# Output weights loaded in parts, one multiplication moved on ScalarE, and a new order at the end, in a fused attention and squared-ReLU kernel

## The chip, the cores and the metric

The kernel runs on one core of one Trainium2 chip, in float32. The metric is the device time of one execution in microseconds (us). A profiled execution gives a trace of every instruction; its span runs from the first instruction of the program to the last.

## The reference

```
# q, k, v: (8, 12, 448, 64); g_q, g_k: (64,)
q_n, k_n = rmsnorm(q, g_q), rmsnorm(k, g_k)       # x / sqrt(mean(x*x) + 1e-6) * g
attn = softmax(q_n @ k_n.T / 8)                    # per batch and head, 448 x 448
x = (attn @ v).transpose(0, 2, 1, 3).reshape(3584, 768)
h = maximum(x @ w_in, 0)                           # w_in: 768 x 2048
out = (h * h) @ w_out                              # w_out: 2048 x 768
```

Eight batches of twelve heads go through attention; their 3584 rows go through a feed-forward network with a squared ReLU.

## The kernel before

**Attention** works on pairs of heads: 48 pairs (six in each batch), two heads of 64 side by side on 128 partitions. For a pair, q and k are scaled by their root mean square, transposed (on TensorE for early pairs; for later ones by block-wise DMA loads and a transpose on VectorE, `turn_blocks`, L364), and q is then multiplied by the gains g on ScalarE (L369). TensorE makes scores (`score`, L429), ScalarE takes exponentials (`weigh`, L451, the instruction is L454), and TensorE multiplies these with v (`attend`, L518, with the matmuls L550 and L571 for late pairs). Late pairs are "whole": they are handled in one visit (`visit_whole`, L1772), in which scores, exponentials and the attend step of the pair before alternate on TensorE and ScalarE.

**The feed-forward network** works in four units `u` of two batches each. Matrix products are done with seven products in place of eight (Strassen's scheme, in Winograd's form). A unit has four blocks; a block has a first product (x times w_in, 128 x 224 pieces, L1042, from unit 1 on with two levels of the scheme, `deep_products`, L1013) and a second product (hidden times w_out, 128 x 384 pieces, L1251, `second_products`, L1205). The second product needs eight "forms" of two tiles of w_out, named 11, 12, 21, 22, T1 to T4; they are made once, in unit 0, kept in DRAM (`out_forms`), and loaded again for each block of units 1 to 3 by `load_out` (L899, the DMA is L902). One load is 128 x 3072 floats, 1536 KB; two make up a block.

The seven products of a row tile are P1 to P7, in an order given by lists (`SECOND_ORDER` and others, L916 on). Each product is added to accumulators by ScalarE or VectorE (`add_to`, L1339, with the addition L1345). P1 and P2 make the upper left part c11, P1, P6, P5 and P3 the upper right c12, P7 adds to both lower parts c21 and c22. After the last block the accumulators are stored by SP (`store`, L1346, the DMA is L1350). Units 1 and 2 ("KEPT", "split") spread their second product over five PSUM banks, and keep 64 rest rows of each batch for unit 3, which handles them as one more row tile, `tt == NT`, the last of four in each block. Their operands come from DRAM by `bring_rests` (L1181).

**The order of the work** is written out by a planner in Python: `ffn` (L943) is a generator that yields after each product with a cost; `run` (L1586) draws from it up to a planned cost, and between draws gives out other work: attention tasks, and DMA issues that were put into `later` with a countdown of steps (`follow_loads`, L1535). `visit_whole` and the visits like it stand between two stretches of `run`. At the end of a unit (`x == unit`, L1851) `drain` gives out all tasks that are left, and then the next unit's generator is begun. [...]nearly all DMAs are issued by SP, in one queue.

Of the kernel before, what the change touches and what calls it, by code (L numbers as in the profile page):

```python
# [225 lines left out]
def program(ctx, tc, rows, v, g, wide, ones, moe_w_in, moe_w_out, out, shift):  # L226

    nc = tc.nc

    B, H, S, D = v.shape  # L230
    NPAIR = H // 2
    DM, DFF = moe_w_in.shape
    NC = DM // P
    NF = DFF // P
# [42 lines left out]
    def whole(i):  # L277
        return i > 2 * 2 * NPAIR
# [30 lines left out]
    def room_for_blocks(i, x):  # L309
        return rows.room(i)[:, x].rearrange("p g h d -> p (g h d)")[:, ds(i % 2 * S, S)]  # L310
# [53 lines left out]
    def turn_blocks(i, x):  # L364
        ensure("blocks", i, x)
        dst = att.tile([P, S], F32, name="qT" if x == 0 else "kT")
        nc.vector.transpose(dst, room_for_blocks(i, x))  # L367
        if x == 0:
            nc.scalar.mul(dst, dst, g)  # L369
        turned[i, x] = dst  # L370

    def load_v(i):
        b, c = pairs[i]
# [321 lines left out]

    def leave(i):
        b, c = pairs[i]
        for x in range(2):
            del turned[i, x]
        del values[i]  # L700
        if b == 1:
            begin_forms(c)
        elif b > 1:
            settle(b, c)
# [191 lines left out]
        side, place = divmod((n * 10 + PLACES[m]) % (2 * SIDE_OF_RING), SIDE_OF_RING)  # L896
        return ring[side][:, place]

    def load_out(n):  # L899
        if NF // 2 <= n < B // 2 * NF // 2:  # L900
            out_sb[n] = new_out()
            nc.sync.dma_start(out_sb[n], out_forms[n % (NF // 2)])  # L902

    roles = [banks[n] for n in (7, 6, 5)]

    def turn_roles(*order):
# [9 lines left out]
    FIRST_ORDER = ["P1", "P5", "P2", "P6", "P3", "P4", "P7"]  # L916
    FIRST_OF_BLOCK = ["P1", "rest0", "P5", "P4", "P6", "P2", "rest1", "P3", "P7"]
    SECOND_ORDER = ["P1", "P2", "P5", "P6", "P4", "P3", "P7"]
    SPLIT_ORDER = [
# [285 lines left out]
    def second_products(u, blk, hid, sums_, accs):  # L1205
# [20 lines left out]
                yield len(some) * COST_OUT  # L1226
            turn_roles(2, 1, 0)

        def store_rows(tt, e):
            if tt is None or tt == NT:  # L1230
                n = u if tt is None else KEPT[e]
                parts = [(2 * n, P * NT, REST), (2 * n + 1, 0, REST)]
            else:
                parts = [(2 * u + e, REST * e + P * tt, P)]
            store(accs[-1] if tt is None else accs_of(tt)[e], parts)

        def accs_of(tt):
            return extra["accs"] if tt == NT else accs[2 * tt : 2 * tt + 2]
# [48 lines left out]
        def store_some(name):  # L1287
            if name in ("P2", "P4") and blk == NBLK - 1:
                while to_store:
                    store_rows(*to_store.popleft())  # L1290

        if split:
            places = [*roles, banks[1], banks[2]]
            for name, tt, n in SPLIT_ORDER:
# [9 lines left out]
                if tt:  # L1304
                    store_some(name)
                yield COST_OUT
        for tt in range(0 if split else NT + final):
            order = SECOND_ORDER if tt or not u else FIRST_OF_BLOCK
            for name in order:
                if name.startswith("rest"):  # L1310
                    a = int(name[-1])
                    multiply_rest(
                        u, blk, hid, banks[2:0:-1], PARTS_BY_ROW[2 * a : 2 * a + 2],
                        accs[-1] if a else None,
                    )
                    if a:
                        held.discard("others")
                    yield 2 * COST_OUT
                    continue
                ps = roles[PRODUCTS[name][0]][:, 0:HALF]  # L1320
                product(tt, name, ps, nc.scalar if order is SECOND_ORDER else nc.vector)
                if name == "P1" and order is FIRST_OF_BLOCK:
                    yield from sums_behind_first()
                    continue
                if order is not FIRST_OF_BLOCK:
                    store_some(name)
                yield COST_OUT
            turn_roles(2, 0, 1)
        while to_store and blk == NBLK - 1:
            some = to_store.popleft()  # L1330
            if final:
                store_rows(*some)
            else:
                later.append([2, lambda some=some: store_rows(*some)])
        for n in ns:
            del out_sb[n]
        later.append([4, lambda: [load_out(n + 2) for n in ns]])

    def add_to(acc, ps, first=False, engine=nc.scalar):  # L1339
        if first and engine is nc.scalar:  # L1340
# [2 lines left out]
            nc.vector.tensor_copy(out=acc, in_=ps)  # L1343
        else:
            nc.vector.tensor_tensor(out=acc, in0=acc, in1=ps, op=ALU.add)  # L1345
    def store(acc, parts):  # L1346

        at = 0
        for b, row, n in parts:
            nc.sync.dma_start(out[ds(b * S + row, n), :], acc[at : at + n, :])  # L1350
            at += n


# [181 lines left out]
    def follow_loads():  # L1535

        for some in to_load:
            some[0] -= 1
        while to_load and to_load[0][0] <= 0:
            load_weights(to_load.popleft()[1])  # L1540
        for some in later:
            some[0] -= 1
        while later and later[0][0] <= 0:
            later.popleft()[1]()

# [224 lines left out]
            tasks.append(lambda: load_blocks(i, 1))  # L1770

    def visit_whole(i):  # L1772
        late = [some for some in tasks if getattr(some, "args", None) == (i,)]
        for some in late:
            tasks.remove(some)
        run_all()
        if shift:
            attend_all(i - 1)
            if i <= last:
                weigh_slots(i, 1)  # L1780
        else:
            if i % 2 == 0:
                both_denominators(i - 2)
            for n in range(NJ):
                attend(i - 1, (n,))
                forget(i - 1, (n,))
                if i <= last:
                    score(i, n)
                    weigh(i, n)
                while n == 1 and i % 2 == 0 and late:  # L1790
                    late.pop(0)()
            if i % 2:
                attend(i - 1, (NJ,))
                forget(i - 1, (NJ,))
            join_halves(i - 1)
            if i % 2 == 0:
                tasks.append(lambda: invert_both(i - 2))
                if i <= last:
                    score(i, NJ)
                    weigh(i, NJ)  # L1800
            if i <= last:
                additions(i)
        tasks.extendleft(reversed(late))
        if late:
            tasks.extendleft([gap] * 3)
        if shift or i % 2:
            prepare(i + 3)
        else:
            tasks.append(lambda: tasks.append(lambda: prepare(i + 3, 0)))
        if i <= last:  # L1810
            tasks.appendleft(lambda: load_v(i))
# [7 lines left out]
    with tc.manual_schedule(engines=ENGINES):  # L1819
        if shift:  # L1820
            rows.scale(0, 1, nc.gpsimd)
        turn(0, 1)
        turn(0, 0)
        for x in range(2):
            rows.normalize_first(1, x, new_acc()[:, 0 : 4 * P])
        if shift:
            rows.scale(1, 1, nc.gpsimd)
        for i in range(len(pairs) + 1):
            for n in range(1 if whole(i) else VISITS):
                at = i * VISITS + n - VISITS - unit  # L1830
                if at < 0:
                    visit_alone(i, n)
                    continue
                u, x = divmod(at, unit)
                if x == 0:
                    u, x = u - 1, unit
                run(place(u, x - (1 if whole(i - 1) else 0.5)))
                if i < last:
                    if whole(i) and not shift:
                        tasks.append(partial(lambda i: turn_blocks(i + 1, 1), i))  # L1840
                        tasks.append(partial(lambda i: turn_blocks(i + 1, 0), i))
                        tasks.append(partial(lambda i: load_qk(i + 4), i))
                    else:
                        for some in (1, 0) if whole(i) else (1 - n,):
                            turn_among(i + 1, some)
                        if n or whole(i):
                            tasks.append(lambda i=i: load_qk(i + 4))
                    if n and first and x > 1 and not shift:
                        denominators(i - 1)
                run(place(u, x))  # L1850
                if x == unit:  # L1851
                    drain()
                    stream, spent, first = ffn(u + 1), 0, u < 0
                    if shift:
                        run(COST if first else LATER)
                    elif first:
                        run(COST_IN + 1)
                slowly = x < unit
                if whole(i):
                    visit_whole(i)  # L1860
                else:
                    visit_among(i, n)
        run(LATER)
        drain()
        assert not transfers
        for _ in ffn(B // 2 - 1):
            follow_loads()
            follow_plan(1)
# [29 lines left out]
```

## Time and profile before

| what | value |
|---|---|
| median of 3 runs | 1393.48 us (1393.12 to 1394.81) |
| the profiled execution's own time | 1394.38 us |
| its span | 1392.6 us |
| TensorE (PE) busy | 1363.3 us, 98% |
| ScalarE (ACT) busy | 608.3 us, 44% |
| VectorE (DVE) busy | 807.2 us, 58% |
| GpSimd (POOL) busy | 789.6 us, 57% |
| moved by DMA | 233.36 MB, mean 168 GB/s |
| granted TensorE clock | 0.998 of full speed |

PE stands for matmuls, PEld for weight loads, SPq for SP's queue of DMA issues. One float32 matmul shows as two records. In a timeline line the first number is the start in us from the span's start, the second how long the line's records lasted together, then engine, line of the kernel, operation, output and inputs with shapes, the number of records, and in brackets how long the engine stood idle before the first and what released it. In the list of costliest groups the numbers behind the bar are busy us, mean ns of one, and idle us before the group. In the list of DMA issues they are the size of one and the median time from issue to landing.

The units end at about 486, 800 and 1102 us; from 1102 us on only the last unit's products run.

### The profile page before, as it was taken

The numbers are of one execution on the slowest core, as the hardware profiler recorded it, in microseconds if no ns is written. First come the engines' busy times: TensorE is split into PE (matmuls) and PEld (weight loads), VectorE is DVE, ScalarE is ACT, GpSimd is POOL, SyncE is SP. The second block draws the span as 40 slices with busy tenths as digits, with TensorE's granted clock in tenths as the row PEclk, the third lists the DMA queues.
The fourth block names the chain that finished last, engine by engine and source line by source line (L and its number), as shares of the span: only waits on it lengthen the run. The fifth ranks groups of instructions, "written<-read, shape, count | busy, mean of one in ns | idle before, by whom it ended". The sixth has DMA issues, their size and how long they took to land.

```text
span 1392.6 us, 19474 instructions
## 1 busy us (share of the span) xinstructions
PE 1363.3 (98%) x6320; PEld 845.7 (61%) x6320; DVE 807.2 (58%) x1635; ACT 608.3 (44%) x1118; POOL 789.6 (57%) x794
## 2 busy tenths in 40 slices
PE   7999999999999999999999999999999999999997
PEld 3333444444444466676758586676768677868684
DVE  4786545867758755555556755455546642445444
ACT  6885477757666244353434244442434032202020
POOL 5668664746656868576667877566745630303030
PEclk9999999999999999999999999999999999999999
DMA  5566746968769875664739475755527442424223
GB/s 147 149 168 169 203 117 159 264 179 219 233 155 284 231 215 162 187 173 141 204 86 279 140 225 149 211 153 176 146 86 239 142 165 103 135 90 149 78 90 100
DMA packets 385588, 233.36 MB, mean 168 GB/s; under 512 B 272452, under 2 KB 354244, under 8 KB 381380
## 3 DMA queue, kind: packets, MB, share of 16 engines
q1 hardware_dynamic: 385184, 231.95, 57.7%
q8 instruction: 52, 0.85, 0.3%
q14 instruction: 60, 0.49, 0.1%
q10 hardware_dynamic: 292, 0.07, 0.0%
HBM read 174.59 MB, written 57.34 MB: 167 GB/s over the span
## 4 chain that ended last, share of the span: by engine, by line
PE 81%; POOL 4%; DVE 4%; DMA 3%; issue 3%; SPq 2%; ACT 2%; POOLq 0%; ACTq 0%; DVEq 0%
PE bank L1251 30%; PE bank L1042 20%; PE bank L986 8%; PE bank L446 5%; PE bank L536 5%; PE bank L550 4%; PE bank L435 4%; PE bank L1165 2%; POOL sum L473 2%; PE bank L585 1%; DMA qk<-in_k_dram 1%; PE bank L611 1%; SPq L326 1%; SPq L318 1%; PE bank L571 1%
## 5 line engine op out<-in xcount | busy, mean ns | idle before, releaser
L1042 PE MATMUL bank<-xT,in_sb 128*128 128x224 f32 x1344 | 289.3, 354 | 2.9 <-ACT part L1031 2.3
L1251 PE MATMUL bank<-out_sb,hid 128*128 128x384 f32 x768 | 272.5, 488 | 2.2 <-POOL out_sb L1514 1.4
L1345 DVE TENSOR_TENSOR acc<-acc,bank 128x384 f32<-128x384 f32 x312 | 166.6, 548 | 164.6 <-PE bank L1251 138.1
L1042 PEld LDWEIGHTS bank<-xT,in_sb 128*128 128x128 f32 x1344 | 252.6, 190 | 15.0 <-ACT wT L454 5.6
L454 ACT ACTIVATE wT<-bank,rr 128x448 f32<-128x448 f32 x288 | 163.5, 631 | 155.1 <-PE bank L435 92.7
L1251 PE MATMUL bank<-out_sb,sums 128*128 128x384 f32 x576 | 207.2, 490 | 1.3 <-DVE acc L1345 0.9
L1251 PEld LDWEIGHTS bank<-out_sb,hid 128*128 128x128 f32 x768 | 144.7, 190 | 104.5 <-issue 5.6
L204 POOL TENSOR_TENSOR rr<-ms,minus_half 128x8 f32<-128x8 f32 (+1 forms) x96 | 146.0, 1521 | 73.7 <-DVE ms L197 63.8
L1251 PEld LDWEIGHTS bank<-out_sb,sums 128*128 128x128 f32 x576 | 107.7, 190 | 86.3 <-issue 4.3
L1027 DVE TENSOR_TENSOR hid<-hid,bank 128x224 f32<-128x224 f32 x312 | 111.0, 383 | 83.9 <-PE bank L1042 79.1
L986 PE MATMUL bank<-xT,in_sb 128*128 128x448 f32 x336 | 131.9, 546 | 0.1
L473 POOL TENSOR_TENSOR sum<-sum,wT 128x448 f32<-128x448 f32 (+1 forms) x96 | 110.6, 1173 | 8.1 <-ACT wT L454 6.6
L986 PEld LDWEIGHTS bank<-xT,in_sb 128*128 128x128 f32 x336 | 62.1, 190 | 69.0 <-issue 60.2
L446 PE MATMUL bank<-qT,kT 64*128 64x448 f32 (+1 forms) x492 | 100.5, 571 | 1.9 <-DVE qT L409 1.1
L473 POOL TENSOR_TENSOR sum<-wT 128x448 f32<-128x448 f32 x48 | 55.8, 1183 | 69.8 <-ACT wT L454 69.8
L1099 ACT ACTIVATE hid<-hid 128x448 f32<-128x448 f32 x96 | 55.0, 573 | 66.7 <-DVE hid L1027 48.5
L435 PE MATMUL bank<-qT,kT 64*64 64x448 f32 x552 | 77.0, 547 | 1.9 <-ACT wT L454 1.9
L1042 PE MATMUL bank<-more,in_sb 128*128 128x224 f32 x288 | 76.2, 357 | 1.4 <-DVE hid L1037 1.4
L550 PE MATMUL bank<-wT,vt 64*64 64x448 f32 x576 | 74.3, 548 | 0.0
L1039 ACT COPY hid<-bank 128x448 f32<-128x448 f32 x24 | 12.8, 532 | 137.3 <-PE bank L1042 137.3
L369 ACT ACTIVATE qT<-qT,g 128x448 f32<-128x448 f32 x34 | 22.6, 665 | 113.7 <-DVE qT L367 113.7
L446 PEld LDWEIGHTS bank<-qT,kT 64*128 64x128 f32 (+1 forms) x492 | 34.9, 166 | 60.4 <-issue 36.8
(140 smaller groups left out, 2059.1 us busy)
## 6 DMA issues: line engine op xcount, KB each, us to landing
out_sb<-out_forms SPq DMA_DIRECT2D x24, 1536.0 KB, 9.9
in_sb<-in_deep SPq DMA_DIRECT2D x64, 384.0 KB, 4.2
in_sb<-in_deep SPq DMA_DIRECT2D x80, 256.0 KB, 4.1
words<-in_moe_w_in_dram SPq DMA_DIRECT2D x32, 384.0 KB, 3.8
words<-in_moe_w_out_dram SPq DMA_DIRECT2D x32, 384.0 KB, 3.6
out_forms<-out_sb SPq DMA_DIRECT2D x8, 1536.0 KB, 7.5
qk<-in_q_dram SPq DMA_DIRECT2D x96, 96.0 KB, 2.6
qk<-in_k_dram SPq DMA_DIRECT2D x96, 96.0 KB, 2.7
```

The source lines that it names most:

```text
L204: self.nc.gpsimd.tensor_tensor(out=self.rr[i][:, x, 0 : self.count(i)], in0=ms, in1=self.minus_half.to_broadcast(list(ms.shape)), op=ALU.pow,)
L435: nc.tensor.matmul(sc[ds(half * D, D)], lhsT=turned[i, 1][ds(e * D, D), ds(m * P + half * D, D)], rhs=turned[i, 0][ds(e * D, D), :], start ...
L446: nc.tensor.matmul(sc[some], lhsT=turned[p, 1][r, keys], rhs=turned[p, 0][r, :], start=True, stop=True,)
L454: nc.scalar.activation(new_weights((i, m), e), sc, AF.Exp, scale=rows.rr[i][:, 1, 2 * m + e : 2 * m + e + 1],)
L473: nc.gpsimd.tensor_tensor(out=sums[i, e][some], in0=left[some], in1=weights[key_of(i, m), e][some], op=ALU.add)
L536: nc.tensor.matmul(values_bank(i)[ds(e * D, D), :], lhsT=lasts[i % 2][mine, e, :] if m == NJ else values[i][:, m, e, :], rhs=weights[key_o ...
L550: nc.tensor.matmul(bank[ds(e * D, D), :], lhsT=values[i][keys, n, e, :], rhs=weights[(i, n), e][keys], start=n == 0, stop=n == NJ - 1 and ...
L986: nc.tensor.matmul(ps, lhsT=w_sb[:, IN.index(left), c, :], rhs=forms[u, c][right], start=first and c == 0, stop=c == NK - 1, skip_group_ch ...
L1027: nc.vector.tensor_tensor(out=quarter(name, n), in0=quarter(base, n), in1=ps, op=ALU.add)
L1042: nc.tensor.matmul(ps, lhsT=left, rhs=right, start=start, stop=stop, skip_group_check=True)
L1251: nc.tensor.matmul(ps, lhsT=extra[left][:, t] if tt == NT else lefts[left][:, t, ts(tt, P)], rhs=w_sb[t][:, OUT.index(right), :], start=fi ...
L1345: nc.vector.tensor_tensor(out=acc, in0=acc, in1=ps, op=ALU.add)
```

## The change

Three edits, independent of each other.

1. `turn_blocks` no longer always issues the multiplication of q by its gains at once. It puts it into a list `to_scale`, which is worked off at once unless `closing` is set. `closing` is set when a unit ends (before `drain`) and the visit that follows is a whole one; that visit issues what is in the list after its exponentials.
2. `load_out` no longer loads all eight forms in one DMA per tile four steps after the block's end. It puts eight loads per block into `forms_to_load`, with countdowns of 4, 7, 10, ... 25 steps, so over the next block's first product: forms 11 and 12 (in units 1 and 2 only 11), T3 and T4, T1 and T2, 21 and 22, each for both tiles.
3. In the last unit each block takes the row tiles in the order 0, NT, 1, 2 in place of 0, 1, 2, NT. The very last row tile takes P7 before P3 (`LAST_ORDER`), stores the left half of its upper rows after P2, its lower rows after P7, and the right half of its upper rows at the end.

```diff
         nc.vector.transpose(dst, room_for_blocks(i, x))
+        turned[i, x] = dst
         if x == 0:
+            to_scale.append(dst)
+            if not closing:
+                scale_turned()
+
+    def scale_turned():
+        while to_scale:
+            dst = to_scale.popleft()
             nc.scalar.mul(dst, dst, g)
-        turned[i, x] = dst
...
-    def load_out(n):
-        if NF // 2 <= n < B // 2 * NF // 2:
+    def load_out(ns):
+
+        unit_of = ns[0] * 2 // NF
+        if not 0 < unit_of < B // 2:
+            return
+        for k, some in enumerate((ds(0, 1 if unit_of in KEPT else 2), ds(6, 2), ds(4, 2), ds(2, 2))):
+            for t, n in enumerate(ns):
+                forms_to_load.append([4 + 3 * (2 * k + t), partial(load_forms, n, some)])
+
+    def load_forms(n, some):
+        if n not in out_sb:
             out_sb[n] = new_out()
-            nc.sync.dma_start(out_sb[n], out_forms[n % (NF // 2)])
+        nc.sync.dma_start(out_sb[n][:, some], out_forms[n % (NF // 2)][:, some])
...
+    LAST_ORDER = ["P1", "P2", "P5", "P6", "P4", "P7", "P3"]
...
-        for tt in range(0 if split else NT + final):
-            order = SECOND_ORDER if tt or not u else FIRST_OF_BLOCK
+        for tt in () if split else (0, NT, 1, 2) if final else range(NT):
+            ends = final and blk == NBLK - 1 and tt == NT - 1
+            order = LAST_ORDER if ends else SECOND_ORDER if tt or not u else FIRST_OF_BLOCK
...
+                if ends and name == "P2":
+                    store_rows(tt, 0, slice(0, HALF))
...
             if final:
-                store_rows(*some)
+                store_rows(*some, slice(0 if some[1] else HALF, DM))
...
-        later.append([4, lambda: [load_out(n + 2) for n in ns]])
+        load_out([n + 2 for n in ns])
...
         while later and later[0][0] <= 0:
             later.popleft()[1]()
+        for some in forms_to_load:
+            some[0] -= 1
+        while forms_to_load and forms_to_load[0][0] <= 0:
+            forms_to_load.popleft()[1]()
...
     def visit_whole(i):
+        nonlocal closing
...
             if i <= last:
                 additions(i)
+        closing = False
+        scale_turned()
...
                 if x == unit:
+                    closing = whole(i)
                     drain()
```

`store` and `store_rows` get an argument for the columns, all of them by default, and `leave` (L696) calls `scale_turned` too.

More of the change, by code (lines that the diff above doesn't have):

```diff
@@ L367, in turn_blocks @@
         nc.vector.transpose(dst, room_for_blocks(i, x))
+        turned[i, x] = dst
         if x == 0:
+            to_scale.append(dst)
[4 more added lines that the diff above has]
+            dst = to_scale.popleft()
             nc.scalar.mul(dst, dst, g)
-        turned[i, x] = dst
+    to_scale, closing = deque(), False
     def load_v(i):
@@ L897, in form_of @@
         return ring[side][:, place]
-    def load_out(n):
-        if NF // 2 <= n < B // 2 * NF // 2:
+    def load_out(ns):
[7 more added lines that the diff above has]
+        if n not in out_sb:
             out_sb[n] = new_out()
-            nc.sync.dma_start(out_sb[n], out_forms[n % (NF // 2)])
+        nc.sync.dma_start(out_sb[n][:, some], out_forms[n % (NF // 2)][:, some])
+    forms_to_load = deque()
     roles = [banks[n] for n in (7, 6, 5)]
@@ L1227, in second_products, with store_rows @@
             turn_roles(2, 1, 0)
-        def store_rows(tt, e):
+        def store_rows(tt, e, columns=slice(None)):
             if tt is None or tt == NT:
@@ L1234, in store_rows @@
                 parts = [(2 * u + e, REST * e + P * tt, P)]
-            store(accs[-1] if tt is None else accs_of(tt)[e], parts)
+            store(accs[-1] if tt is None else accs_of(tt)[e], parts, columns)
         def accs_of(tt):
@@ L1320, in second_products @@
                 ps = roles[PRODUCTS[name][0]][:, 0:HALF]
-                product(tt, name, ps, nc.scalar if order is SECOND_ORDER else nc.vector)
+                product(tt, name, ps, nc.vector if order is FIRST_OF_BLOCK else nc.scalar)
                 if name == "P1" and order is FIRST_OF_BLOCK:
@@ L1345, in add_to, with store @@
             nc.vector.tensor_tensor(out=acc, in0=acc, in1=ps, op=ALU.add)
-    def store(acc, parts):
+    def store(acc, parts, columns=slice(None)):
         at = 0
         for b, row, n in parts:
-            nc.sync.dma_start(out[ds(b * S + row, n), :], acc[at : at + n, :])
+            nc.sync.dma_start(out[ds(b * S + row, n), columns], acc[at : at + n, columns])
             at += n
@@ L1802, in visit_whole @@
                 additions(i)
+        closing = False
+        scale_turned()
         tasks.extendleft(reversed(late))
```

## The prediction

> **What bounds the kernel now.** I read the busy times first, then TensorE's idle time by place (timeline of PE), then what ACT, SP and DVE did at those places.
>
> ```profile
> PE 1363.3 (98%) x6320; PEld 845.7 (61%) x6320; DVE 807.2 (58%) x1635; ACT 608.3 (44%) x1118; POOL 789.6 (57%) x794
> ...
> PE   7999999999999999999999999999999999999997
> ...
> L369 ACT ACTIVATE qT<-qT,g 128x448 f32<-128x448 f32 x34 | 22.6, 665 | 113.7 <-DVE qT L367 113.7
> ...
> out_sb<-out_forms SPq DMA_DIRECT2D x24, 1536.0 KB, 9.9
> in_sb<-in_deep SPq DMA_DIRECT2D x64, 384.0 KB, 4.2
> ```
>
> TensorE is busy 1363.3 of 1392.6 us; no change to its 6320 matmul records is in the diff, so only the other 29.3 us, and time in which records are busy but held up, can go. In the timeline the 29.3 us are 9.5 us before 21 us (first loads), 7.5 us after the last matmul, and 12.3 us in some 25 gaps of at most 1.9 us. The largest of those, and its surroundings, on PE and then on ACT:
>
> ```profile
> 486.33 0.98 PE L550 MATMUL bank<-wT,vt 64*64 64x448 f32 x8
> 487.13 0.93 PE L435 MATMUL bank<-qT,kT 64*64 64x448 f32 x8
> ...
> 491.44 0.59 PE L435 MATMUL bank<-qT,kT 64*64 64x448 f32 x2 [1.89 <-ACT wT L454]
> ...
> 496.29 0.65 PE L1042 MATMUL bank<-xT,in_sb 128*128 128x224 f32 x2
> ```
>
> ```profile
> 490.20 0.67 ACT L369 ACTIVATE qT<-qT,g 128x448 f32<-128x448 f32 x1 [6.06 <-DVE qT L367]
> 490.77 2.44 ACT L454 ACTIVATE wT<-bank,rr 128x448 f32<-128x448 f32 x4
> ```
>
> The same visit of an odd pair one unit later:
>
> ```profile
> 800.23 0.98 PE L550 MATMUL bank<-wT,vt 64*64 64x448 f32 x8
> ...
> 805.87 0.65 PE L1042 MATMUL bank<-xT,in_sb 128*128 128x224 f32 x2
> ```
>
> The reader is to see that 800.23 to 805.87 is 5.64 us, and 486.33 to 496.29 is 9.96 us for the same 56 matmul records. The other ten such visits take 5.61 to 5.67. So 4.32 us are lost here, more than the 1.89 us gap. The cause stands on ACT: the multiplication L369 waits for DVE's transpose, 6.06 us idle, and the exponentials L454, whose scores were ready from about 488.1 (487.13 + 0.93), stand behind it.
>
> The other two places are a weight DMA and the end:
>
> ```profile
> 532.32 1.37 PE L1042 MATMUL bank<-xT,in_sb 128*128 128x224 f32 x6 [0.57 <-DMA in_sb<-in_deep]
> ```
>
> ```profile
> 499.82 2.02 SPq L902 DMA_DIRECT2D out_sb<-out_forms  x2
> ...
> 503.98 6.98 SPq L326 DMA_DIRECT2D qk<-in_k_dram  x4
> 511.06 3.19 SPq L326 DMA_DIRECT2D qk<-in_q_dram  x2
> ```
>
> ```profile
> 1384.40 3.58 SPq L1350 DMA_DIRECT2D out_dram<-qk  x4
> 1385.11 1.02 DVE L1345 TENSOR_TENSOR qk<-qk,bank 128x384 f32<-128x384 f32 x2 [0.73 <-PE bank L1251]
> ```
>
> After two 1536 KB loads SP needs 6.98 us for four issues that take about 0.5 each elsewhere. At the end two DVE additions follow the last product, then two stores.
>
> [...]ACT sat 6.06 us with ready exponentials behind one waiting multiplication. [...]eight L435 records take 0.93 us when issued together, and in the disturbed visit pairs of them take 0.59 to 0.96, which is why the loss exceeds the gap. [...]the trace's output stores took 2.3 to 4.0 from issue to landing. [...]the 1.02 us of the two big issues on SP are no measure of the load; the 9.9 us to landing is.
>
> **The change, part by part.**
>
> *1. q's factors behind the exponentials.* Set side by side, the ACT streams of the two kernels differ, apart from accumulator names in the last unit, by one instruction: the multiplication of 490.20 now stands behind six exponentials and the two copies L561, L562. At the second unit's end (800.09) it stays where it is: it ran before `closing` was set, and no scores waited there (exponentials at 802.00 waited for PE). Nothing else holds the exponentials: they wait for PE (488.1) and for POOL additions that read the same wT buffers, done by about 482. So the visit goes from 9.96 to about 5.64: 4.32 us. Cost: L562 ends 1.1 us after the first L1042 matmul, the multiplication (0.67, its transpose was done at 490.16) comes next, and the copy L1039, which in the like visit idled 0.28 before starting, moves 0.67 - 0.28 = 0.4 us later; the next use of that bank follows on its heels (498.31 here, copy's end 498.26), so PE pays 0.4. Net 3.9 us; bounds 1.5 (only the gap, less the 0.4) and 4.3. What is late next: POOL runs on without a break from 488.30 to about 499, but its result for step 2 of the deep products (495.4) is needed some 7.6 us after they start, about 499.6. No stall.
>
> *2. Forms in parts.* Before: per block two loads of 1536 KB at step 4. After: eight, of 384 KB (in units 1 and 2 the first two of 192 KB)[...]; units 1 and 2 leave out form 12, which they don't use (16 x 192 KB, 3 MB of 233). SP gets 6 more issues per block, at 0.4 to 0.5 us about 2.7 us in some 75 us, beside PE; against this go the stalls of 6.98 - 4 x 0.5 = 5 and 3.19 - 1 = 2 us. Of TensorE's waits only the 0.57 us at 532.32 is for a DMA behind this hump (its issue at 528.56 waited for no semaphore, SP was merely late; by my count it now issues about 519.5 where 524 would do). Gain 0.57; bounds 0 and 0.6.
> The parts come later than the whole did. Taking for each the issue times of its unchanged neighbours in SP's stream, and for its need the first product that reads it, the slack is 7.1 us in the tightest case (block 3 of unit 1, last part beside the issue at 765.54, product P2 at 772.66), 7.7 in block 0 (T1 at 530.45 for 538.15), over 8 elsewhere in units 1 and 2, and 13 in the last unit. A 384 KB load lands in 4.2 us (median above)[...]. Cost 0; bounds 0 and 1.
>
> *3. New order at the end.* In all blocks of the last unit the rest rows come second. PE has no listed wait from 1085 us on (300.07 busy of 301.00), the products are the same, and their operands come earlier than needed: cost 0. In the last block the order P7, P3 leaves one DVE addition (0.55) after the last matmul instead of two (1.02): 0.47 us. Then one store of 128 x 384 instead of two of 64 x 768: the second's issue began at 1386.67, 0.51 after the first, and landed 3.63 after that, at 1390.30; lone 128-row stores of the same block landed 2.3 to 2.7 us after their issue. PE ends at 1385.07 here; the new store is issued 0.6 later and should land at +3.2 (0.6 + 2.6, since a 384 KB store is issued 0.8 us ahead of it), where the old one landed at +5.23. The 2.28 us from landing to the span's end stay. Gain 2.0; bounds 1.3 and 2.5. The half stored after P2 has the five products behind it, 5 x 1.29 = 6.5 us, to land.
>
> Sum: 3.9 + 0.6 + 2.0 = 6.5 us. The profiled execution took 1394.38 (span 1392.6 and 1.8 around it), so 1387.9 for its like; it lies 0.9 over the median of the runs, 1393.48, from which I get 1387.0.
>
> **The rivals.**
> - *Only the visible gap goes.* If the visit keeps its broken pairs, or POOL or SP take back what it gains: 1.5 + 0.6 + 1.5 = 3.6, 1389.9. For it: two thirds of the loss show as busy. Against: eleven undisturbed visits within 0.06 us of each other.
> - *The parts free more.* The gaps after 500 us sum to 6.9; without the 0.57 they end on ACT and DVE work whose order is unchanged. If a third were due to late small loads: another 2.1, 1384.9.
> - *It doesn't do what it says.* Gains are eaten by stalls of under 1 us at two thirds of the eight blocks of units 1 and 2: near 1392, no measurable change.
> - *Slower: the last part is late.* In the built SP stream every DMA issue waits for the landing of the one eight issues before, so one slow load holds up all behind it. If the last parts needed what the whole needed (issue 500.58, landing 512.23: 11.65 us), the blocks of units 1 and 2 would wait 3.9, 1.6, 0, 4.5, 3.2, 1.4, 0, 0 = 14.6 us (11.65 less the slack of each), and the time would be 1387.0 + 14.6 = 1401.6. Waits begin above 7.1 us; the gain is gone at about 10. Against it: the 11.65 us belong to 3 MB at once.
>
> **How the numbers follow.** Forecast 0.72, with its own range 1385.6 to 1388.4 (bounds of the three terms, and 0.7 of scatter between runs); only the gap 0.12; more freed 0.07; no net change 0.05; late parts 0.04. A measurement of this kernel can tell about 0.2%, 2.8 us, from no change. Faster by more than that (below 1390.7): 0.72 + 0.11 + 0.07 = 0.90; same 0.06; slower 0.04. The range 1384.5 to 1390.0 takes in the first three cases.
>
> **What would show it.** Right: the visit at about 486 takes 5.6 to 6.1 us with its exponentials from 488.1 and the multiplication behind L562; no wait of PE for in_sb near 528; no issue of SP over 2 us behind the forms; after the last matmul one DVE addition and a span end 5.3 to 5.9 us later instead of 7.5. Wrong: PE waits for out_sb<-out_forms at P2 or P5 of units 1 and 2, or an exponential at 488 that waits for POOL.

## The result, and the profile after

The changed kernel takes 1388.98 us (median of 7 runs, 1388.10 to 1389.66) where the kernel before takes 1393.9 on the same chip: ratio 0.9962, interval 0.9953 to 0.9971. Beside the experiments it was measured twice more: 1387.5 (0.9961, 0.9947 to 0.9975) and 1387.61 (0.9958, 0.9944 to 0.9971). So it gains 4.9 to 5.7 us; the forecast was a gain of 6.5 and a time of 1387.0, with a range of its own from 1385.6 to 1388.4, so the first measurement lies 0.6 above that range. The profiled execution took 1389.2, its span is 1387.2 us. One of the 13 executions of a later experiment, without the parts, took 3140.09 us and is in no ratio.

The busy times and the two kinds of weight loads, as the page of the changed kernel has them:

```profile
PE 1361.1 (98%) x6320; PEld 845.3 (61%) x6320; DVE 806.2 (58%) x1635; ACT 608.5 (44%) x1118; POOL 790.0 (57%) x794
...
out_sb<-out_forms SPq DMA_DIRECT2D x80, 384.0 KB, 5.1
in_sb<-in_deep SPq DMA_DIRECT2D x64, 384.0 KB, 4.0
```

The work is the same. The 24 big loads have become 96 (80 of 384 KB and 16 of 192 KB), and a 384 KB part lands 5.1 us after its issue (median). Now the visit at the first unit's end, the timeline of PE and then of ACT (lines have moved: the exponentials are L463, the multiplication by g is L377, the deep products L1064):

```profile
486.77 0.98 PE L559 MATMUL bank<-wT,vt 64*64 64x448 f32 x8
487.58 0.93 PE L444 MATMUL bank<-qT,kT 64*64 64x448 f32 x8
...
492.47 0.65 PE L1064 MATMUL bank<-xT,in_sb 128*128 128x224 f32 x2
```

```profile
488.63 1.16 ACT L463 ACTIVATE wT<-bank,rr 128x448 f32<-128x448 f32 x2 [4.04 <-PE bank L444]
...
493.07 0.56 ACT L571 COPY xT<-bank 128x448 f32<-128x448 f32 x1
493.50 0.70 ACT L377 ACTIVATE qT<-qT,g 128x448 f32<-128x448 f32 x1
494.07 0.55 ACT L1061 COPY hid<-bank 128x448 f32<-128x448 f32 x1
```

The visit takes 492.47 - 486.77 = 5.70 us instead of 9.96; the exponentials wait for PE's scores alone, and the multiplication stands behind the copies. Next, PE where it waited 0.57 us for in_sb before, and then its only new wait:

```profile
526.54 1.19 PE L1064 MATMUL bank<-more,in_sb 128*128 128x224 f32 x4
527.57 1.68 PE L1064 MATMUL bank<-xT,in_sb 128*128 128x224 f32 x8
529.08 1.45 PE L1273 MATMUL bank<-out_sb,hid 128*128 128x384 f32 x4
```

```profile
768.23 0.81 PE L1273 MATMUL bank<-out_sb,hid 128*128 128x384 f32 x2
769.80 0.88 PE L1273 MATMUL bank<-out_sb,hid 128*128 128x384 f32 x2 [0.76 <-DMA out_sb<-out_forms]
```

The first wait is gone: the eight records at 527.57 run through. The second is P2 of block 3 of unit 1, the block that the prediction called tightest: its last part was issued at 765.71 and landed at 769.67. Last, DVE at the end:

```profile
1380.43 1.02 DVE L1370 TENSOR_TENSOR acc<-acc,bank 128x384 f32<-128x384 f32 x2 [0.74 <-PE bank L1273]
1381.72 0.56 DVE L1370 TENSOR_TENSOR acc<-acc,bank 128x384 f32<-128x384 f32 x1 [0.27 <-PE bank L1273]
```

One addition follows the last matmul (it ends at 1381.68), and the span ends at 1387.2: 5.5 us later instead of 7.5.

The two spans differ by 5.4 us. By place this is: the visit -4.26, the in_sb wait -0.57, the end -2.0, the out_sb wait +0.76, the later copy +0.18. That makes -5.9; the other +0.5 I take for scatter, which is not shown for all of it (PE already stood 0.67 us later at 463 us, ahead of anything that the change touches).

### The profile page after: what moved, and what is told of

The parts are those of the page before. It is cut to its first block, busy times and chain, and to the rows that moved or that the text cites. A ratio compares the mean times of both kernels' runs of the same rounds, so it can differ in the third digit from the quotient of the medians.

```text
span 1387.2 us, 19565 instructions
## 1 busy us (share of the span) xinstructions
PE 1361.1 (98%) x6320; PEld 845.3 (61%) x6320; DVE 806.2 (58%) x1635; ACT 608.5 (44%) x1118; POOL 790.0 (57%) x794
## 4 chain that ended last, share of the span: by engine, by line
PE 82%; POOL 7%; issue 3%; DVE 2%; ACT 2%; DMA 2%; SPq 1%; POOLq 0%; DVEq 0%; ACTq 0%
PE bank L1273 31%; PE bank L1064 21%; PE bank L1008 8%; PE bank L559 4%; PE bank L444 4%; PE bank L455 4%; PE bank L545 4%; POOL sum L482 2%; PE bank L1187 2%; POOL sums L1173 1%; PE bank L620 1%; PE bank L594 1%; PE bank L611 1%; POOL rr L204 1%; PE bank L580 1%
## 5 line engine op out<-in xcount | busy, mean ns | idle before, releaser
L1064 PE MATMUL bank<-xT,in_sb 128*128 128x224 f32 x1344 | 289.0, 354 | 2.3 <-ACT part L1053 2.3
L1064 PEld LDWEIGHTS bank<-xT,in_sb 128*128 128x128 f32 x1344 | 252.7, 190 | 14.0 <-ACT wT L463 5.6
L463 ACT ACTIVATE wT<-bank,rr 128x448 f32<-128x448 f32 x288 | 163.6, 631 | 159.6 <-PE bank L444 97.6
L1117 POOL TENSOR_TENSOR hid<-hid 128x448 f32<-128x448 f32 x24 | 27.2, 1139 | 123.3 <-DVE hid L1049 118.9
L1064 PE MATMUL bank<-more,in_sb 128*128 128x224 f32 x288 | 76.1, 357 | 1.4 <-DVE hid L1059 1.4
```

Of the source, the lines that this page charges most:

```text
L463: nc.scalar.activation(new_weights((i, m), e), sc, AF.Exp, scale=rows.rr[i][:, 1, 2 * m + e : 2 * m + e + 1],)
L1064: nc.tensor.matmul(ps, lhsT=left, rhs=right, start=start, stop=stop, skip_group_check=True)
```

## The experiments

Each kernel was run beside the kernel before on the same chip. The first four take the three edits apart.

**The factor alone.** "The factor" is short for edit 1, the multiplication of q by its gains behind the exponentials. Edit 1 stays, edits 2 and 3 are undone:

```diff
-        load_out([n + 2 for n in ns])
+        later.append([4, lambda: [load_out(n + 2) for n in ns]])
...
-        for tt in () if split else (0, NT, 1, 2) if final else range(NT):
+        for tt in () if split else range(NT + 1) if final else range(NT):
-            ends = final and blk == NBLK - 1 and tt == NT - 1
+            ends = False
```

(with `load_out` as before, and the last stores whole).

> The kernel before with only q's multiplication moved behind the exponentials. My theory: the visit at 486 us falls from 9.96 to about 5.7 us, less 0.2 to 0.4 for the late copy: 3.9 us faster than before, ratio about 0.9972. Rival (only the visible gap of 1.89 us counts): 1.5 us, ratio 0.9989. PE keeps its 0.57 us wait for in_sb, and the span ends 7.5 us after the last matmul.

Measured: 1395.18 us, ratio 1.0019 (1.0010 to 1.0028): slower than before. PE's timeline of this kernel (the deep products are L1053 here), then the same spot one unit later, and a table of windows, that is, of stretches of a few us (busy us of PE, PEld, DVE, ACT, POOL, then TensorE's granted clock, DMA share, GB/s):

```profile
530.49 2.58 PE L1053 MATMUL bank<-xT,in_sb 128*128 128x224 f32 x6 [3.07 <-DMA in_sb<-in_deep]
532.87 1.83 PE L1262 MATMUL bank<-out_sb,hid 128*128 128x384 f32 x4
...
842.55 1.37 PE L1053 MATMUL bank<-xT,in_sb 128*128 128x224 f32 x6 [1.38 <-DMA in_sb<-in_deep]
843.76 1.45 PE L1262 MATMUL bank<-out_sb,hid 128*128 128x384 f32 x4
```

```profile
526.00:530.00 4.00, 1.42 (x7) 0.78 (x5) 0.94 (x4) 2.89 (x7) 2.26 (x2) 1.00 0.72 221
530.00:534.00 4.00, 3.51 (x9) 2.89 (x10) 0.69 (x2) 1.00 (x2) 3.88 (x4) 0.57 1.02 343
```

The visit does take 5.70 us, and PE is then 4.3 us ahead of the kernel before. At 530.49 that is gone, in two ways. PE comes to the in_sb tile at 527.4 and stands 3.07 us, where it stood 0.57 before. And then its granted clock is 0.57 on the mean of 530 to 534 us, which is 3.4 us at half clock: the same six records take 2.58 us here and 1.37 at 842, the next four 1.83 and 1.45. Sum: 3.07 - 0.57 = 2.5 of waiting, and 1.6 in these ten records, together 4.1 of the 4.3. The 1.38 at 842 comes on top. Other executions had more half clock than this one: its mean granted clock is 0.998, that of eight of the eleven is 0.996 or 0.997. The load's history stands in SP's timeline:

```profile
499.43 1.74 SPq L912 DMA_DIRECT2D out_sb<-out_forms  x2
501.27 1.03 SPq L902 DMA_DIRECT2D in_sb<-in_deep  x2
502.39 7.96 SPq L326 DMA_DIRECT2D qk<-in_k_dram  x4
510.46 3.09 SPq L326 DMA_DIRECT2D qk<-in_q_dram  x2
...
526.18 2.44 SPq L902 DMA_DIRECT2D in_sb<-in_deep  x5
```

Behind the two loads of 1536 KB, six small issues hold SP for 11 us, and everything behind them in the queue is late, up to the in_sb load: the second of the five at 526, issued at 526.81, landed at 530.36. PE goes on 0.13 later. The landing sets the time, not PE: in the four traces with whole loads (before, this one, the end alone, without the parts) it comes at 532.18, 530.36, 530.28 and 532.10, while PE gets there at 531.75, 527.42, 530.16 and 527.26. A faster PE only waits longer. What holds SP is only in part known: 6.10 of the 11 us are one issue (503.51 to 509.61), and the DMA eight issues before it had landed at 502.43, so the waiting rule that the prediction's last rival names does not explain that one. (The rule itself holds: in the trace of before, of 932 issues for which the landing of the one eight before is known, none ended ahead of it; with seven before, 32 of 933 did.)

**The parts alone**: `scale_turned` is called at once, and edit 3 is undone.

> The kernel before with only the output forms loaded in parts. My theory: the wait of 0.57 us for in_sb goes, a wait of about 0.8 us for out_sb comes in block 3 of unit 1: net 0.3 us slower, ratio 1.000 within 0.0005, so the change's second part bought nothing. Rival (the parts free small loads everywhere): 1 to 2 us faster, ratio 0.999.

Measured: 1392.92 us, ratio 0.9997 (0.9988 to 1.0005). The in_sb wait is gone, and the wait for out_sb in block 3 of unit 1 came, but with 0.21 us and not 0.8. The visit still has its 1.89 us gap, so PE comes to the in_sb tile late, and the 0.57 was all that there was to win.

**The end alone**: `scale_turned` at once, `load_out` as before.

> The kernel before with only the new order of the last unit and the last stores in halves. My theory: 2.0 us faster, all of it after the last matmul (7.5 us to the span's end become 5.5), ratio 0.9986. Rival (the last store is bound by its landing whatever its shape, so only the one addition of 0.47 us goes): ratio 0.9997.

Measured: 1391.46 us, ratio 0.9994 (0.9987 to 1.0000). By the time alone this is nearer to the rival's 0.9997 than to the 0.9986 of the theory; the trace has more. PE's last matmul ends at 1383.24, the span at 1388.7: 5.5 us. The two experiments with the old end have 6.8 and 6.9, the kernel before 7.5, so the new end is worth 1.3 to 2.0, more than the one addition of 0.47. This trace also has the undisturbed price of the visit. PE over it (its deep products are L1052), then the windows, of the kernel before and then of this one:

```profile
486.60 0.98 PE L558 MATMUL bank<-wT,vt 64*64 64x448 f32 x8
...
491.71 0.59 PE L443 MATMUL bank<-qT,kT 64*64 64x448 f32 x2 [1.89 <-ACT wT L462]
...
494.87 0.65 PE L1052 MATMUL bank<-xT,in_sb 128*128 128x224 f32 x2
```

```profile
486.00:492.00 6.00, 4.11 (x38) 1.44 (x40) 4.03 (x8) 1.80 (x4) 5.92 (x7) 1.00 0.50 109
492.00:496.00 4.00, 4.00 (x28) 1.35 (x20) 0.00 (x0) 2.10 (x4) 3.92 (x5) 0.57 0.43 80
```

```profile
486.00:492.00 6.00, 4.11 (x35) 1.36 (x37) 4.30 (x8) 1.53 (x3) 5.92 (x6) 1.00 0.48 99
492.00:496.00 4.00, 4.00 (x34) 2.10 (x27) 0.02 (x1) 3.58 (x7) 3.92 (x6) 1.00 0.49 98
```

Both have the gap, but before's clock was halved behind it (granted 0.50 from 492.18 on, for 3.41 us, 0.57 on the mean of the window) and this one's was not (1.00). Its visit takes 486.60 to 494.87, 8.27 us, as with the parts alone (487.63 to 495.90). So of the 4.3 us that the factor takes away in the trace of before, 8.27 - 5.70 = 2.6 are order on ACT, and 1.7 are the half clock of that one execution.

**Without the parts**: edits 1 and 3 stay, `load_out` is as before.

> The changed kernel with the forms loaded whole again, so parts 1 and 3 of the change alone. My theory: the sum of these two, 5.9 us faster than before, ratio 0.9958, so as fast as or 0.3 us faster than the changed kernel (0.9962). Rival (the parts are needed once the visit is short, because PE then meets the two big loads): 0.5 to 1 us slower than the changed kernel, ratio 0.9967 or more, with waits of PE for in_sb after 496 us.

Measured: 1393.28 us, ratio 1.0007 (0.9999 to 1.0016). Two edits that seemed worth 5.9 us together give nothing. PE again, and the windows around the wait:

```profile
532.24 2.58 PE L1053 MATMUL bank<-xT,in_sb 128*128 128x224 f32 x6 [4.98 <-DMA in_sb<-in_deep]
```

```profile
526.00:530.00 4.00, 1.26 (x6) 0.68 (x4) 0.77 (x3) 2.89 (x7) 2.39 (x3) 0.91 0.58 110
530.00:534.00 4.00, 1.76 (x5) 1.65 (x6) 0.00 (x0) 0.84 (x2) 3.77 (x4) 0.50 0.97 331
534.00:540.00 6.00, 6.00 (x20) 4.00 (x19) 3.17 (x7) 1.43 (x3) 0.14 (x1) 0.83 0.96 330
```

A lead of 4.5 us becomes a lag of 1.8: 4.98 - 0.57 = 4.4 longer wait, and 6.8 us of half clock (0.91, 0.50 and 0.83 on the means of the three windows), of which 3.8 lie behind the wait and cost 1.9. The theory that the edits simply add up has fallen. The wait for in_sb that takes the gain's place is what the rival said, but its size was not: the rival had 0.5 to 1 us over the changed kernel (0.9967 or somewhat more), and it is about 6.

The next four run together on another chip, the changed kernel among them.

> The changed kernel once more, to stand beside the three below on the same chip. Both theories: about 1389.0 us, 0.9962 of the kernel before; TensorE's wait for out_sb at about 770 us (0.76 in the first profile) again, between 0.5 and 1.0, no wait for in_sb at 530 and none at 843.

Measured: 1387.5 us, ratio 0.9961 (0.9947 to 0.9975). The wait at 770 is 0.32 here, less than the 0.5 to 1.0 that were expected, and the others are absent.

**Parts sooner**:

```diff
-                forms_to_load.append([4 + 3 * (2 * k + t), partial(load_forms, n, some)])
+                forms_to_load.append([4 + 2 * (2 * k + t), partial(load_forms, n, some)])
```

> The changed kernel with the parts of the forms two visits apart instead of three; in the built stream of SP the last part of block 3 of unit 1 then goes out about 8.5 us sooner (beside 757.2 instead of 765.7). Theory (the 0.76 us wait at 770 is a part that comes late): the wait is gone, about 1388.2 us, 0.8 below the changed kernel. Rival (parts that come sooner crowd SP before the in_sb loads, as the whole loads did): a wait for in_sb of 0.5 to 2 us comes at about 530 or 843, and the time is 1389 to 1391.

Measured: 1388.02 us, ratio 0.9960 (0.9947 to 0.9974). The wait at 770 is gone, as the theory says, and no wait for in_sb came. The time is that of the changed kernel: the 0.8 us that the theory promised beside it are not seen; what is left to win there, 0.3 to 0.8, is less than runs differ by.

**Last parts later**:

```diff
-                forms_to_load.append([4 + 3 * (2 * k + t), partial(load_forms, n, some)])
+                forms_to_load.append([4 + 3 * (2 * k + t) + (3 if k == 3 else 0), partial(load_forms, n, some)])
```

> The changed kernel with the last two parts of every block three visits later. In the built stream of SP they move by 2 to 7 us in units 1 and 2; in block 3 of unit 1, where TensorE already waits 0.76 us, by 2.3 (765.7 to 768.0). Theory (only that block is near its limit): its wait grows to about 3.1 us and no other block waits; 2.3 more than the changed kernel, 1391.3, or 1393.0 if TensorE's clock is halved for 3.4 us after such a wait, as it was after the 3.07 us wait in the trace with the factor alone. Rival (the slower case of the forecast: little slack in all eight blocks): waits in three blocks or more, 1395 or above.

Measured: 1393.68 us (13 runs, 1389.91 to 1394.83), ratio 1.0003 (0.9995 to 1.0011): the whole gain of the change is gone, with two loads of each block moved by a few us. Its trace, of the shortest execution, has one wait of 2.02 us at 770, in block 3 of unit 1 and in no other, and full clock; 3.1 us had been expected. It was run once more, beside the changed kernel on a third chip:

> The kernel with the last parts three visits later, once more, for its slower executions: it took 1389.9 to 1394.8 before, and the one profile was of the fastest. Theory (the wait at 770, 2.02 us, lowers TensorE's clock to half for 3.41 us[...]): a trace of about 1392 to 1394 us shows a half-clock stretch right after a wait at 770, and each such stretch costs up to 1.7 us. Rival: the slower executions have longer or more waits for out_sb, and full clock.

Measured: 1391.9 us (10 runs, 1389.56 to 1394.89), ratio 0.9988 (0.9979 to 0.9997), where the changed kernel has 0.9958: most of the gain is gone, not all. This time the profiled execution was a long one (1394.31, span 1392.5). PE and the windows behind it:

```profile
768.67 0.88 PE L1273 MATMUL bank<-out_sb,hid 128*128 128x384 f32 x2 [1.00 <-DMA out_sb<-out_forms]
772.25 1.62 PE L1273 MATMUL bank<-out_sb,hid 128*128 128x384 f32 x2 [2.69 <-DMA out_sb<-out_forms]
```

```profile
768.00:772.00 4.00, 0.88 (x2) 0.30 (x2) 1.04 (x2) 0.00 (x0) 4.00 (x5) 0.86 0.96 280
772.00:776.00 4.00, 3.75 (x14) 1.01 (x18) 1.24 (x3) 0.00 (x0) 1.68 (x3) 0.50 0.49 104
776.00:780.00 4.00, 4.00 (x38) 1.82 (x34) 1.31 (x3) 1.31 (x3) 0.00 (x0) 0.79 0.32 82
```

Both sides were half right: both tiles' parts came late (1.00 + 2.69 instead of 2.02), and the granted clock was 0.86, 0.50 and 0.79 in these windows: 6.8 us at half clock, from 770.88 on. One other block waits as well, with 0.58 us at 614. The prediction costed such waits at their length. Here 3.69 us of waiting and the half clock behind it cost PE 6.8 us: it starts the visit at the second unit's end at 801.87, the changed kernel on this chip at 795.09, and ahead of the wait the two were level (766.22 and 766.20).

**Parts in one block**: the forms are loaded in parts in block 0 of unit 1, and whole in the other eleven blocks.

```diff
+        if ns[0] != NF // 2:
+            forms_to_load.extend([4, partial(load_forms, n, ds(0, 8))] for n in ns)
+            return
         for k, some in enumerate((ds(0, 1 if unit_of in KEPT else 2), ds(6, 2), ds(4, 2), ds(2, 2))):
```

> The changed kernel with the forms in parts in block 0 of unit 1 only; in the other eleven blocks each of the two loads of 1536 KB is whole again, at step 4. Theory (the parts are worth something in one place above all: they let SP issue the in_sb load of about 528 us in time, and so let the gain of the factor stand): no wait for in_sb at 530, none for out_sb at 770 (0.8 less), and at about 843, where the trace with the factor alone shows a wait of 1.38, that wait again: 1389.0 - 0.8 + 1.4 = 1389.6 us. Rival (the parts help by less crowding in many blocks): nearer to the kernel with the factor and the new end but no parts, which took 1.0007 of the kernel before: 1391.5 to 1393.5.

Measured: 1387.54 us, ratio 0.9957 (0.9944 to 0.9971): all of the gain. SP's timeline at the place where it stood 11 us, and PE at the in_sb tile:

```profile
500.31 1.52 SPq L902 DMA_DIRECT2D in_sb<-in_deep  x2
501.88 0.42 SPq L924 DMA_DIRECT2D out_sb<-out_forms  x1
502.40 1.95 SPq L326 DMA_DIRECT2D qk<-in_k_dram  x4
504.45 2.27 SPq L326 DMA_DIRECT2D qk<-in_q_dram  x2
```

```profile
526.81 1.68 PE L1067 MATMUL bank<-xT,in_sb 128*128 128x224 f32 x8
```

No wait at 530 and none at 770. The 1.38 at 842 that was expected didn't come either: at that place the load landed at 835.56, just ahead of its use. With the kernel without any parts (1.0007) this settles the parts: of the twelve blocks only this one needs them.

The last three are about the end, on the third chip.

> The changed kernel beside the three below. 1387.5 to 1389 us; from the end of TensorE's last matmul to the end of the span 5.4 to 5.5 us, as in its two earlier traces.

Measured: 1387.61 us, ratio 0.9958 (0.9944 to 0.9971); 5.4 us from the last matmul to the end. In this third trace of the changed kernel PE has no wait at 770.

**Lower rows first**:

```diff
-    LAST_ORDER = ["P1", "P2", "P5", "P6", "P4", "P7", "P3"]
+    LAST_ORDER = ["P1", "P5", "P6", "P4", "P7", "P2", "P3"]
...
                     store_some(name)
+                if ends and name == "P7":
+                    store_some("P4")
                 if ends and name == "P2":
```

(The order is that of the very last row tile alone, not of three as the expectation says.)

> The changed kernel with the products of its last three tiles of rows in the order P1 P5 P6 P4 P7 P2 P3, so that the lower rows of the last tile (384 KB) are stored two products (2.6 us) sooner and only 192 KB, one product ahead, go out before the last store. Theory (the last store landed 3.9 us after its issue instead of the forecast 2.6 because a 384 KB store was 0.8 us ahead of it): it lands in 2.6 to 3.1, and the end comes 4.7 to 5.0 us after the last matmul, 0.5 to 0.8 below the changed kernel. Rival (the last store takes what it takes, alone or not): 5.4 again and no difference.

Measured: 1387.14 us, ratio 0.9955 (0.9942 to 0.9969). The last store landed 3.3 us after its issue instead of 3.8, and the span ended 5.2 us after the last matmul: 0.3 less, below the 0.5 to 0.8 that were expected and not to be seen in the times.

The last experiment has two of these edits in one, parts in block 0 of unit 1 only and the lower rows first:

> Two edits to the changed kernel that looked free or useful: the forms in parts in block 0 of unit 1 only, and the lower rows stored first at the end. Both theories of the parts: as fast as the changed kernel or faster; if the lower rows are worth what is expected of them, 0.5 to 0.8 less, 1386.8 where the changed kernel takes 1387.5.

Measured: 1387.46 us, ratio 0.9961 (0.9947 to 0.9974); 5.1 us at the end again. No version is measurably faster than the changed kernel.

## Why the prediction was right, and where not

**The sum** held within 0.8 to 1.6 us (a gain of 4.9 to 5.7 where 6.5 was forecast), and it came out of the right places of the trace. The first measurement, 1388.98, is 2.0 over the forecast and 0.9 under the rival in which only the gap goes; the two others are 0.5 and 0.6 over it, but on chips where the kernel before was up to 0.7 us faster than the prediction's 1393.48. The prediction's own range is narrower at its upper end than the bounds of the three gains: these add up to 2.8 to 7.4, which is 1386.1 to 1390.7. The split of the sum did not hold, and that the sum did is in part luck: step 1 was priced too high and step 2 far too low, and both edits were in the change. The edits can be made one by one, but their gains are not independent.

**Step 1, 3.9 us.** The visit fell to 5.70 as forecast (5.64), the exponentials start at 488.63, POOL held nothing up, and the later copy costs 0.18 instead of 0.4 (the words product starts at 494.67; by the spacing before it 494.49). But 1.7 of the 4.3 us were half clock in the execution that was profiled, and what is order on ACT is 2.6 (8.27 - 5.70). The prediction put the whole excess over the gap to broken pairs, which cost 0.7 where the clock is full (8.27 - 5.64 - 1.89). It also called that excess two thirds of the loss; 2.43 of 4.32 is little over half. The clock row of the page has one digit for a fortieth of the span (35 us) and hides a stretch of 3.41 us; a window of a few us shows it.

Such stretches are no rarity where the visit is the old one. One like that of the trace of before takes 3.41 / 2 / 1393 = 0.0012 off the mean clock. The kernel before has a mean of 0.998 or less in 43 of its 81 executions beside the experiments, the changed kernel in none of 17, but this is not a clean count: the clock is also halved behind the last matmul (granted 0.50 from 1389.89 to the end in the trace of before, 2.7 us, and from 1386.87 in the trace after, 0.3 us), and the old end leaves more room for that. The kernel with the end alone has the old visit and the new end, and there the mean is 0.998 in 8 of 21 executions. So part of the 1.7 is gained, but not in each run.

**Step 2, 0.57 us, is the step that failed.** It was costed as the wait that stands in the trace of before, with step 1 beside it as if the two were independent. With PE 4.3 us earlier, the same late load would have been waited for 3 to 5 us, with half clock on top (3.07 and 4.98 us in the two traces that have it, with 3.4 and 6.8 us of half clock); the parts are what let step 1 stand. By themselves they gave nothing that can be measured (0.9997), on top of edits 1 and 3 they turn 1.0007 into 0.9958 to 0.9962, which is 6 to 7 us. The numbers for this were in the working: an in_sb load issued at 528.56, and step 1 that brings its need forward by 4.3. The step even used the earlier need for the question whether the load would now be in time: its 524 fits the old need of 531.75 less 4.3 and less a landing of 3.6; without the 4.3 it would be 528. It did not use it for what the edit is worth. The new issue was counted as 519.5; it is 522.40, lands at 526.37, and is needed at 527.95. 1.6 us of slack are left, not 4.5. (A slip without effect: in the line that the prediction shows, the two big issues take 2.02 us on SP, not 1.02.)

The cost of the late parts, 0 (bounds 0 and 1), measured 0.76, 0.32 and nothing in the three traces of the changed kernel, in the block that was named. By the prediction's own list this wait at a P2 is a sign of being wrong; it is small beside the 14.6 us of that rival. The slack of 7.1 us there less a landing of 4.0 should have left 3; the part was issued at 765.71 for a product that was now due at 769.0, since PE had come 3.6 us earlier and SP had not. Here the slacks were counted without what step 1 moves. The rival with late parts priced waits at their length. It had the gain gone when landings take about 10 us, which by its slacks is 6 to 7 us of waiting in three blocks; in the two traces with the last parts later, 2.02 us at full clock made an execution of 1389.91 us, and 3.69 with the clock halved behind it one of 1394.31, with nothing left of the gain.

**Step 3, 2.0 us.** The end fell from 7.5 to 5.5 us in the two profiled executions, with one addition, as forecast. Over all traces the old end takes 6.8 to 7.5 and the new one 5.4 to 6.0 (without the two kernels that store the lower rows first), so 1.5 is the better number. The landing took 3.8 to 3.9 us and not 2.6; what stood between landing and end was shorter, 1.0 instead of 2.28. Landings are inferred, so only the distance from the last matmul to the end is sure. A 384 KB store 0.8 us ahead of the last one explains 0.5 to 0.9 of the longer landing (3.3 and 2.9 us in the two kernels with the lower rows first), not all.

One kernel was not run: edits 2 and 3 without edit 1. That the factor gives some 4 us on top of them follows only from the others (0.9997 x 0.9994 against 0.9958 to 0.9962), if edits 2 and 3 add up.

## What to carry to other kernels

When an engine is made earlier at one place, walk on from there through every transfer that it needs, with its need moved forward, before counting the gain; a short wait behind the place (0.57 us here) is a limit that the gain runs into (it became 3.07 and 4.98), and an edit that looks worthless alone may be what pays. Big loads can cost what stands behind them in the queue (here six small issues took 11 us behind two of them): split the one whose followers are due, and leave the rest. And look at the clock in windows of a few us where TensorE stood (here half clock came with waits of 1.89 us and more), before taking a stretch of one execution for the price of an order of instructions.

## What the hardware showed that was not expected

TensorE's granted clock fell to 0.50 in the middle of a kernel in which it is 98% busy, in four of these traces: for 3.41 us in the trace of before, from 492.18 on, behind a wait of 1.89 us; for 3.4 us with the factor alone, at a wait of 3.07; for 6.8 us without the parts, at a wait of 4.98; and for 6.8 us in the second trace with the last parts later, at waits of 1.00 and 2.69. Two waits of 1.89 us (the parts alone, the end alone) and one of 2.02 (the first trace with the last parts later) left it at full speed. So the length of a wait did not settle it by itself: 1.89 us came with half clock in one execution and without it in two, and 2.02 without it. What else decides, these traces do not show. What the 3.41 us cost they do: the same visit took 9.96 us with them and 8.27 without, 1.7 more.
